# Gate and up halves of the narrow Strassen products in one PSUM bank, evicted and joined together, with a new written list of steps

## The chip, the cores and the metric

One core of a Trainium2 chip runs the whole program in one launch. The metric is the device time in microseconds, the median over runs. The change is compared with the kernel before on the same chip.

## The reference

The input is x, 2048 tokens of 512 features, with one layernorm. The output is x plus two branches of the normed tokens:

```python
xn = _layernorm(x, axis=-1)
return x + _A_ref(xn, A_wqkv, A_w_phi, A_wo) + _B_ref(xn, B_w_gate, B_w_up, B_w_down)

def _A_ref(x, wqkv, w_phi, wo):               # 32 heads of 16
    pq = jnp.einsum("bhsd,hdf->bhsf", q, w_phi)
    ...
    phi_q = jnp.concatenate([_softmax(pq, axis=-1), _softmax(-pq, axis=-1)], axis=-1)
    phi_k = jnp.concatenate([_softmax(pk, axis=-1), _softmax(-pk, axis=-1)], axis=-1)
    kv = jnp.einsum("bhsf,bhsd->bhfd", phi_k, v)
    z  = jnp.einsum("bhsf->bhf", phi_k)
    o = jnp.einsum("bhqf,bhfd->bhqd", phi_q, kv) / (phi_q . z + 1e-6)
    return o @ wo
def _B_ref(x, w_gate, w_up, w_down):          # 512 -> 1792 -> 512
    g = jnp.einsum("bsd,df->bsf", x, w_gate)
    u = jnp.einsum("bsd,df->bsf", x, w_up)
    return jnp.einsum("bsf,fd->bsd", g * u, w_down)
```

## The kernel before, in words

**Tokens and stages.** The 2048 tokens are 16 tiles of 128, four to a group of 512. After a fixed start (layernorm of tiles 0 to 3, their values, the first hidden columns) everything is a named step. The steps of every engine stand in one list, the string `ORDER`, written out by hand; the program issues them in exactly that order, and the place in each PSUM and SBUF ring is written out beside it (`SLOTS`). Nothing is scheduled at run time: each engine executes its own steps in list order and waits on semaphores.

**Names of steps.** `vk`, `q`, `kx`, `qy`, `kr` and the like are the attention projections and feature maps; `kv{n}` sums keys and values; `ab{n}` is numerator and denominator of a tile, followed by `de`, `rd` and `ot` (denominator, its reciprocal, the scaled tile `otok`, L658) and by `oT`, a DMA that transposes it. `f{n}.{i}` are the pieces of the last projection of a tile, `fs` its eviction and `fo` its store. `P1` to `P8`, `K`, `A`, `B`, `J`, `X` are the same for pairs of tiles in groups 2 and 3 (two lots of Strassen products, with `K` evictions, `J` joins at L991 and stores `X`). `S` and `t`, `wt`, `ct` prepare sums and differences that those products need.

**The hidden products.** Group 0 computes gate and up plainly (`g`, `u`, L351). For the other groups the product of tokens and gate/up weights is done by a seven-product Strassen form over halves of the features, the columns and the tokens. `block_steps(b, group)` makes the steps: block b holds one gate (b even) or one up (b odd) column pair, `k = b // 2`. For tokens 1024 to 2047 it is the wide form (512 columns to a product, steps `p1.b` to `p7.b`). For tokens 512 to 1023 it is the narrow form, with the same names behind an `N` and 256 columns to a product; it covers 14 blocks. Each product is two matmuls (L825).

In one block: product 1 fills bank `sa`, `k1` (L833) evicts it to SBUF, product 6 goes on accumulating in the same bank, `k2` evicts it, product 7 follows, `k3` evicts it, then product 4, which `d4` takes out. Products 2 and then 5, 7, 3 use banks `sb` and `sc`. The joins `j2`, `j7`, `j3` add a bank and a kept copy. In gate blocks a join writes the hidden tile `hT` (L840) and scales by `gate_scale`; in up blocks it writes `u_sb` (L844), and a step `m` multiplies that into `hT` (L847). So a gate block and its up block evict, join and multiply one after the other. A narrow product fills half of a bank; `sa` and `sc` are of the two-deep pool `f` that `=f` opens when the attention pool of `ab` closes (`bank_f`), `sb` is of the ring of six banks (`bank`).

**Engines.** The end of a word says the engine: `/a` ScalarE (ACT), `/v` VectorE (DVE), `/g` GpSimd (POOL). Joins are on the DVE. DMA triggers (`xt`, `qt`, `oT`, `fo`, `X`, `wq`) are all in the SyncE (SP) queue. Where a DVE step and a POOL step both work in SBUF, the POOL step that follows in the list waits for the DVE step (L1064 to L1084).

Of the kernel before, what the change touches and what calls it, by code (L numbers as in the profile page):

```python
# [30 lines left out]
ki4 sc12 h8 u11 vk7.0 vk7.1 kr6 ki6 n0.2 vc6/a ky5 kp4/g vc5/a kx5 kr5 xt10 n2.4 ky7 kx7 wq h11 ki5 kr7 kv4 n0.1
vk8.0 ki7 kp6/g vk8.1 vk10.0 vk10.1 g5 ky8 kx8 kp5/g kp7/g a13/a kv5 vc7/a kr8 xt11 kv6 vk9.0 vk9.1 kx10 ky10
gc5/a vc10/a vc8/v g2 kv7 ki8 a12/v kp8/g kr10 ki10 vc9/a ky9 kx9 Nz0/v fq0 xt13 a14/v vk11.0 vk11.1 fqv0/a
fqa0/a gc2/a ky11 xt12 kx11 kp10/g kv8 fq2 kr9 ki9 fqa2/v u2 q0.0 fqv2/a q0.1 kr11 ki11 qx0 qy0 q1.0 h2 q1.1
kp9/g qy1 kp11/g vk12.0 kv9 vk12.1 xt14 qx1 a15/a vc11/a kx12 kv10 ky12 qr0 qi0 qp0/g n0.6 vk13.0 vk13.1 vk14.0
# [5 lines left out]
qr4 qp5/g inv0 de2 z0/v rd2 f1.0 f1.5 f0.8 qt5 qi4 t00/g ot2 qp4/g z1/g f0.4 oT2 qx6 qy6 qy7 up60/a qr6 ab3 de3
fs0 qx7 rd3 qi6 ot3 qr7 t01/v z2/v n2.1 t02/v qp6/g f2.6 f2.1 f2.2 f2.3 p1.1 f1.6 k1.1/a f1.7 n2.0 ab5 p2.1 p1.0
f2.5 qt4 de5/a rd5 f3.0 p6.1 k1.0/a p6.0 f2.7 j2.1 f2.8 f1.8 qi7 ot5 up11/a k2.0/a t03/v p7.0 ab4 qp7/g oT3 fs2
fo0 Nz2/g q13.0 q13.1 de4/v up10/a t10/g z3/g qt6 fs1 rd4 k2.1/a wr2 p7.1 wf2 ot4 oT5 k3.0/a qx13 qy13 f3.8 qr13
qt7 p4.0 q8.0 p2.0 j2.0 ab6 p5.1 k3.1/a up50/a p4.1 de6/a rd6 p5.0 q8.1 j7.1 ot6 d4.0/a oT4 j7.0 f3.5 ab7 Np2.0
f3.7 de7/v rd7 ot7 p3.1 p3.0 up30/a qy8 up31/a m7.1/g =f t11/v qx8 j3.0 Np1.0 p1.2 Np1.1 Nk1.0/a Np6.0 j3.1
k1.2/a p2.2 Np2.1 Nj2.0 Nz3/g t12/g Nk2.0/a Nk1.1/a Nj2.1 qi13 j2.2 Np7.0 wp2 Nk3.0/a Np6.1 up20/v Nm2.1/v
m3.1/v Nk2.1/a p6.2 Np4.0 Np7.1 q9.0 Nd4.0/a Np5.0 p1.3 Nj7.0 d4.1 Nk3.1/a p2.3 Np4.1 k2.2/a k1.3/a qp13/g Np3.0
Nj3.0 p7.2 up21/a q9.1 k3.2/a Np5.1 Nd4.1 j2.3 p6.3 k2.3/a t13/g Nj7.1 p5.2 p5.3 Np1.2 qx9 Nm7.1/g fs3 Nk1.2/a
p7.3 Np2.2 Np3.1 Np6.2 p4.2 j7.2 p3.2 m2.1/v k3.3/a ws2 Nj3.1 Np1.3 j7.3 Nj2.2 t20/g m2.3/v Nk2.2/a qy9 t22/v  # L50
j3.2 Np7.2 qr8 Nk3.2/a p4.3 Nk1.3/a d4.2/a p2.4 Np4.2 Nd4.2/a Nm3.1/g t21/g t23/g Np6.3 p3.3 p1.4 Np5.2 Nj7.2
d4.3 Nk2.3/a Np7.3 p5.5 p2.5 j3.3 Np3.2 up51/a q10.0 q10.1 Nj3.2 Nk3.3/a m7.3/v up41/a k1.4/a Np5.3 p1.5 m3.3/v
Np4.3 S0.0/g t32/g j2.4 qx10 qy10 Nd4.3 Nj7.3 p6.4 k1.5/a p1.6 Np2.3 qr10 Nm7.3/v j2.5 k2.4/a Nj2.3 p6.5 Np1.4
Np3.3 p7.4 S1.0/g k2.5/a Nj3.3 p7.5 p5.4 Nm2.3/g t30/g Np2.4 k3.4/a p4.4 Nk1.4/a k3.5/a j7.4 Nj2.4 Np6.4 Np5.4
j7.5 Nk2.4/a p3.4 Np2.5 Np7.4 d4.4/a Nm3.3/v t31/g Nk3.4/a ct1.1/a p3.5 m7.5/g Np4.4 p4.5 j3.4 Nd4.4/a k1.6/a
j3.5 Nj7.4 d4.5 qi8 m2.5/v p2.7 p1.7 k1.7/a Np1.5 Np3.4 p6.6 Nj3.4 Nk1.5/a p6.7 Np6.5 k2.6/a Nk2.5/a t33/g Np5.5
Nj2.5 k2.7/a j2.7 p2.6 Np7.5 Nm2.5/v m3.5/v j2.6 S0.2/g Nk3.5/a Nj7.5 p7.6 p7.7 up40/a Np4.5 Nd4.5 k3.6/a m2.7/v
k3.7/a qp8/g Nm7.5/g oT6 p5.6 p5.7 j7.6 Np3.5 Nj3.5 Np1.6 Np2.7 Nk1.6/a p4.6 p3.6 Np6.6 Np2.6 Np1.7 j7.7 j3.6
Nj2.6 qt13 fo1 p4.7 p3.7 t40/v d4.6/a Nm3.5/v Nk1.7/a Nk2.6/a t41/v Np6.7 Np7.6 oT7 Nj2.7 m7.7/g t43/g ct2.0/a
q14.0 p1.8 Nk2.7/a p2.8 Nk3.6/a Np4.6 k1.8/a q14.1 qr9 j2.8 Nd4.6/a Np7.7 Np5.6 qi10 p1.9 p2.9 t42/g Nm2.7/g  # L60
Nj7.6 j3.7 Np3.6 Nj3.6 qx14 Nk3.7/a k1.9/a qy14 p6.8 k2.8/a j2.9 S3.0/g p6.9 Np4.7 m2.9/g Np5.7 Nd4.7 Nj7.7
k2.9/a d4.7 p7.8 p5.8 Np2.8 Np3.7 k3.8/a ct1.0/a Nm7.7/g j7.8 Np1.8 p7.9 Np2.9 Nk1.8/a p3.8 Nj3.7 Np1.9 Np6.8
p5.9 m3.7/v qp10/g k3.9/a Nk1.9/a Nj2.8 j3.8 Nj2.9 Nk2.8/a cb11.0/a j7.9 Nm3.7/v t50/v p1.11 Np7.8 p2.11 Np6.9
Nk3.8/a p3.9 Nm2.9/v wt1.0/v p4.8 Nk2.9/a Np7.9 Np4.8 t52/g t51/g j3.9 qt8 k1.11/a d4.8/a q12.0 q12.1 Nd4.8/a
Nk3.9/a p4.9 Np4.9 Np5.8 qr14 j2.11 p1.10 p2.10 p1.12 Nj7.8 Nd4.9 up61/a qx12 d4.9 wt2.0/g Np1.10 Np3.8 p5.10
m3.9/v k1.10/a Nk1.10/a Np6.10 t53/g Nj3.8 qy12 Np5.9 p2.12 j2.10 Nk2.10/a Nj7.9 m7.9/v Np7.10 t60/v Np2.10
k1.12/a Nk3.10/a Np3.9 p6.10 Np4.10 p6.11 Nj3.9 k2.10/a Nd4.10/a Nj2.10 j2.12 m2.11/g Np5.10 p7.10 q15.0 Np1.12
t62/v t61/v Nj7.10 qi9 p6.12 Np2.12 Nm7.9/g k3.10/a p4.10 Np3.10 qp9/g j7.10 qi14 Nk1.12/a k2.11/a p7.11 Nj2.12
Nj3.10 ct2.1/a p3.10 Np6.12 q11.0 S2.3/g qr12 q15.1 k3.11/a Nk2.12/a d4.10/a qy15 qx15 j3.10 Np1.11 Np7.12 t63/v
S2.2/v S0.4/v Nk1.11/a q11.1 p5.11 Np2.11 Nj2.11 j7.11 p4.11 Np6.11 Nk3.12/a Np4.12 Nd4.12/a k2.12/a d4.11 f4.7  # L70
p2.13 Nk2.11/a Np5.12 qp14/g p3.11 p7.12 qx11 qy11 Np7.11 Nj7.12 Np3.12 f6.0 Nk3.11/a qi12 S0.3/v m7.11/v qt9
f6.8 Nj3.12 j3.11 p1.13 k1.13/a k3.12/a S1.3/g Np4.11 wt2.1/v Nm2.11/v m3.11/v S2.1/v Nm3.9/g f4.2 f4.0 f6.1
Np5.11 Nd4.11 Nj7.11 qp12/g Nm7.11/g p5.12 inv1 p4.12 j2.13 Np1.13 Np3.11 j7.12 Nj3.11 qt14 Nk1.13/a d4.12/a
f6.2 f6.3 p6.13 Np6.13 p3.12 Np2.13 f4.3 k2.13/a Nk2.13/a Np7.13 Nk3.13/a Np5.13 f6.5 p7.13 qr15 S0.1/v S2.4/v
Np4.13 qt12 Nm3.11/g j3.12 Nj7.13 Nm7.13/v Nd4.13 m2.13/v S1.1/v p5.13 k3.13/a ct2.2/a f7.0 f7.1 f6.6 cb11.1/a
# [5 lines left out]
P6a.8 P5a.8 ab13 P5b.8 cb21.1/a f5.7 P2w.9 P6b.9 ct3.1/v S3.4/v oT12 fo4 qt15 oT8 fo6 P6b.8 P6b.11 P2a.9 P2b.9
A1.9/v K5.8/a K6.8/a de13/a wt3.0/v wt3.1/v P7a.8 P7b.8 f5.8 K7.8/a K6.9/a wt4.2/v J2.9 wt4.3/g A1.8/g A6.8/g
P8w.8 rd13 P5a.9 P4b.8 P4w.8 P7a.9 ot13 fs5 S3.6/v wt4.0/v ab10 oT13 fo5 S3.2/v S3.1/v P2w.8 A7.8/g P4a.8 P2a.8
P7b.9 J4.8 J8.8 de10/v K7.9/a P1b.10 B6.8/g S3.5/v rd10 A1.11/v ot10 P1a.10 P2b.8 J2.8 oT10 P3w.8 P3a.8 P3b.8
J3.8 qp11/g qt11 X8 P5b.9 A6.9/v K1.10/a K6.11/v P4w.9 P3w.9 ab15 de15/a rd15 K5.9/a A7.9/g P4b.9 X12.1 X12.0
B6.9/v ot15 P3a.9 P2b.10 P7a.11 P3b.9 P6a.10 P6b.10 P8w.9 P7b.11 K6.10/v J3.9 P4a.9 P2a.10 ab11 K7.11/a de11/a
A1.10/v J8.9 J4.9 P5a.10 P2w.10 J2.10 P3w.10 P5b.10 P3a.10 P3b.10 P4a.11 K5.10/a A6.11/g A7.11/g A6.10/g P5a.11
P5b.11 oT15 rd11 ot11 P2b.11 oT11 P4w.11 B6.10/v J3.10 K5.11/v X13.0 X10 P3a.11 P8w.10 P8w.11 X9 X13.1 B6.11/v
# [1028 lines left out]
```

## Time and profile before

| | |
|---|---|
| median of 3 runs | 211.46 us (211.44 to 211.54) |
| the profiled execution: its time, its span | 211.99 us, 210.3 us |
| PE, DVE, ACT, POOL busy | 205.2, 188.0, 152.4, 139.2 us |
| matmuls | 1463 |
| granted TensorE clock | 1.00 |
| DMA | 19.95 MB in 47,685 packets, mean 95 GB/s |

The profile is one execution. Its span is 1.7 us shorter than its own time, and that time is 0.5 us above the median of the runs. Busy PE counts a matmul to a modelled end that overlaps the next one, so short stops of the PE show only in the starts.

### The profile page before, as it was taken

Reading aid. Unit: us, or ns where it says so; the run is one execution under the profiler, and the core shown is the slowest. Engines: PE = TensorE matmul, PEld = TensorE weight load, DVE = VectorE, ACT = ScalarE, POOL = GpSimd, SP = SyncE. Lnnn points to the kernel's source line nnn. Section 1 sums busy time; section 2 is a strip of 40 time slices with the busy share of each in tenths; the row PEclk is TensorE's granted clock in tenths of the full one; section 3 lists DMA queues with packets and bytes.
Section 4 is the critical chain, followed back from the end, with each engine's and each line's share of the span. In section 5 each row is a group of like instructions: output and inputs, shape, how many; then the busy total and the mean of one; then the engine's idle time right before and its main releaser. Section 6 shows DMA issues by size and latency. Waiting matters only on the chain.

```text
span 210.3 us, 4230 instructions
## 1 busy us (share of the span) xinstructions
PE 205.2 (98%) x1463; PEld 119.8 (57%) x1463; DVE 188.0 (89%) x389; ACT 152.4 (72%) x296; POOL 139.2 (66%) x138
## 2 busy tenths in 40 slices
...
GB/s 160 261 273 380 384 315 108 86 91 53 25 61 67 0 126 99 104 145 32 15 90 0 0 3 50 0 3 3 50 50 59 19 25 125 130 75 77 77 100 75
DMA packets 47685, 19.95 MB, mean 95 GB/s; under 512 B 37424, under 2 KB 47408, under 8 KB 47536
## 3 DMA queue, kind: packets, MB, share of 16 engines
...
q8 instruction: 11, 0.18, 0.4%
q14 instruction: 10, 0.08, 0.2%
HBM read 8.67 MB, written 2.10 MB: 51 GB/s over the span
## 4 chain that ended last, share of the span: by engine, by line
PE 92%; DMA 4%; SPq 1%; DVE 1%; issue 0%; ACT 0%; DVEq 0%; ACTq 0%
PE sa L825 18%; PE fin L682 15%; PE sc L825 9%; PE q L337 7%; PE k L337 7%; PE pv L337 6%; PE u L351 6%; PE g L351 6%; PE da L962 6%; PE sb L825 4%; DMA out_dram<-o_sb 2%; DMA vk<-in_A_wqkv_dram 2%; PE dc L962 2%; PE ab L631 2%; PE kv L594 2%; PE dd L962 2%
## 5 line engine op out<-in xcount | busy, mean ns | idle before, releaser
L563 POOL TENSOR_TENSOR phik<-e,rs 128x1024 bf16<-128x1024 f32 x16 | 30.8, 1935 | 12.8 <-DVE rs L558 9.9
L553 DVE TENSOR_REDUCE sums<-e 128x64 f32<-128x1024 f32 x32 | 38.4, 1200 | 0.8 <-ACT e L541 0.4
L563 POOL TENSOR_TENSOR phiq<-e,rs 128x1024 bf16<-128x1024 f32 x16 | 30.9, 1935 | 8.4 <-DVE dK L985 1.4
L825 PEld LDWEIGHTS <-T 128*128 128x128 f16 x224 | 21.7, 98 | 15.8 <-issue 0.8
L682 PE MATMUL fin<-wd,hT 128*128 128x512 bf16 x112 | 29.4, 379 | 0.0
L357 ACT COPY k<-sa 128x512 f32<-128x512 f32 (+1 forms) x42 | 19.8, 481 | 7.4 <-PE sa L825 4.7
L359 ACT ACTIVATE k<-sa 128x512 f32<-128x512 f32 (+1 forms) x42 | 20.4, 493 | 5.0 <-PE sa L825 2.6
L825 PEld LDWEIGHTS <-wgu 128*128 128x128 bf16 x168 | 16.1, 98 | 13.0 <-DVE otok L658 0.4
L337 PEld LDWEIGHTS <-x 128*128 128x128 f16 x144 | 13.3, 98 | 13.0
L351 PEld LDWEIGHTS <-wgu 128*128 128x128 bf16 x128 | 12.3, 98 | 11.9
L558 DVE RECIPROCAL rs<-sums 128x64 f32<-128x64 f32 x32 | 17.3, 542 | 1.2
L847 POOL TENSOR_TENSOR hT<-u_sb,hT 128x256 f16<-128x256 bf16 (+1 forms) x16 | 13.1, 824 | 7.9 <-DVE wgu L932 4.3
L337 PE MATMUL pv<-vk,x 128*128 128x512 bf16 x48 | 18.2, 379 | 0.0
L337 PE MATMUL k<-vk,x 128*128 128x512 bf16 x48 | 18.2, 379 | 0.0
L682 PEld LDWEIGHTS <-hT 128*128 128x128 bf16 (+1 forms) x112 | 10.5, 98 | 9.9
L825 PE MATMUL sa<-ss,T 128*128 128x512 f16 x56 | 15.8, 379 | 0.0
L840 DVE SCALAR_TENSOR_TENSOR hT<-sc,k 128x512 f16<-128x512 f32 (+1 forms) x28 | 15.3, 545 | 0.5 <-ACT k L357 0.3
L844 DVE TENSOR_TENSOR u_sb<-sc,k 128x512 bf16<-128x512 f32 (+1 forms) x28 | 15.0, 541 | 0.3 <-POOL hT L847 0.2
L711 ACT ACTIVATE junk<-wgu 128x1024 bf16<-128x1024 bf16 x14 | 14.9, 1075 | 0.2 <-DMA x<-xn 0.2
L359 ACT ACTIVATE wgu<-wgu,up 128x1024 bf16<-128x1024 bf16 x13 | 14.9, 1158 | 0.0
L351 PE MATMUL u<-xnT,wgu 128*128 128x512 bf16 (+1 forms) x64 | 14.1, 353 | 0.0
L541 ACT ACTIVATE e<-k 128x512 f32<-128x512 f32 x24 | 13.3, 612 | 0.9 <-PE k L337 0.7
...
## 6 DMA issues: line engine op xcount, KB each, us to landing
...
xall<-in_A_x_dram SPq DMA_DIRECT2D x1, 1024.0 KB, 12.1
...
```

What stands on the lines that cost most here:

```text
L337: nc.tensor.matmul(ps, lhsT=xt(n)[:, j, :], rhs=w[:, j, :], start=(j == 0), stop=(j == DC - 1))
L351: nc.tensor.matmul(ps, lhsT=w[:, c, f * P:(f + 1) * P], rhs=(x4 if T else xnT)[:, c, lo:hi], start=(c == 0), stop=(c == DC - 1))
L357: A.copy(out=dst, in_=src)
L359: A.activation(out=dst, in_=src, func=AF.Identity, scale=scale)
L553: V.tensor_reduce(out=sums[:], in_=ev(), axis=AX.X, op=ALU.add)
L558: V.reciprocal(out=rs[:].rearrange("p a b -> p (a b)"), in_=held.pop((s + "s", n))[:])
L563: eng.tensor_tensor(out=phi[:].rearrange("p g (x f) -> p (g x) f", f=DH), in0=ev(), in1=held.pop((s + "i", n))[:].to_broadcast((P, 2 * H, ...
L682: nc.tensor.matmul(held["fin", n, lo], lhsT=l, rhs=r, start=len(done) == 1, stop=len(done) == FC + DC)
L825: nc.tensor.matmul(mine[bankname], lhsT=ww[:, j, :], rhs=xx[:, j, :], start=start and j == 0, stop=(j == hc - 1), skip_group_check=True)
L840: V.scalar_tensor_tensor(out=h(*to), in0=mine[ps], scalar=gate_scale, in1=mine[kept][:], op0=ALU.mult, op1=ALU.add)
L844: V.tensor_tensor(out=mine["u", i][:], in0=mine[ps], in1=mine[kept][:], op=ALU.add)
L962: nc.tensor.matmul(mine[ps][:, 0:W], lhsT=l, rhs=r, start=bool(mine.pop((ps, "new"), False)), stop=True, skip_group_check=True)
```

## The change

The narrow products are taken by column pair k, gate and up together, in a function of their own, `narrow_steps(k)`. A product is four matmuls: two into the left half of a bank (gate) and two into the right half (up). One eviction, one join and one `d4` of 512 elements replace two of 256 each; the joined tile `gu` holds both halves, and `Nm` multiplies one half by the other into `hT`. `Nd4` writes `gu` too, so it has an `Nm4` of its own. The levels of the two weight scales go from 8 and 8 to 4 and 4, so `gate_scale` is 1 and goes from the wide steps too: gate joins become a plain addition and gate evictions a plain copy. `u_sb` is float16. The list of steps is written anew (1156 words in place of 1247), and with it the places in the rings.

```diff
-    levels = (8.0, 8.0, 4096.0)
+    levels = (4.0, 4.0, 4096.0)
     hidden_scale = 16.0
-    gate_scale = hidden_scale / (levels[0] * levels[1])
...
+    def narrow_steps(k):
+        hc, n = DC // 2, TT // 2
+        cols = pair_cols(k)
...
+        def product(p, bankname, w, x, start=False):
+            def run():
+                if start:
+                    mine[bankname] = (bank if bankname == "sb" else bank_f)(bankname)
+                ww, xx = w(), x()
+                for g in range(2):
+                    for j in range(hc):
+                        nc.tensor.matmul(mine[bankname][:, g * n:(g + 1) * n], lhsT=ww[:, g, j, :], rhs=xx[:, j, :],
+                                         start=start and g == 0 and j == 0, stop=(j == hc - 1), skip_group_check=True)
...
+        def keep(name):
+            def run(eng):
+                mine[name] = ring(xnpool, "x", [P, TT], F32, name)
+                copy(eng, mine[name][:], mine["sa"])
...
+        def both(i):
+            mine["gu", i] = ring(gpool, "g", [P, 2, n], F16, "gu")
+            return mine["gu", i][:].rearrange("p g t -> p (g t)")
...
+        def times(i, t, f):
+            def run(eng):
+                gu = mine["gu", i]
+                eng.tensor_tensor(out=hT(1)[:, k + f * FH, t * n:(t + 1) * n], in0=gu[:, 0], in1=gu[:, 1], op=ALU.mult)
...
+        def join(i, t, f, ps, kept):
+            def run():
+                V.tensor_tensor(out=both(i), in0=mine[ps], in1=mine[kept][:], op=ALU.add)
...
+        steps[f"Nd4.{k}"] = (lambda eng: copy(eng, both(4), mine["sa"]), A)
+        times(4, 1, 0)
```

In the wide steps:

```diff
-                copy(eng, mine[name][:], mine["sa"], gate_scale if g == 0 else None)
+                copy(eng, mine[name][:], mine["sa"])
...
-                if g == 0:
-                    V.scalar_tensor_tensor(out=h(*to), in0=mine[ps], scalar=gate_scale, in1=mine[kept][:],
-                                           op0=ALU.mult, op1=ALU.add)
-                else:
-                    mine["u", i] = ring(gpool, "g", [P, n], BF16, "u_sb")
-                    V.tensor_tensor(out=mine["u", i][:], in0=mine[ps], in1=mine[kept][:], op=ALU.add)
+                if g:
+                    mine["u", i] = ring(gpool, "g", [P, TT], F16, "u_sb")
+                V.tensor_tensor(out=mine["u", i][:] if g else h(*to), in0=mine[ps], in1=mine[kept][:], op=ALU.add)
```

Places of the two lists that matter below, one of before and two of after. A word such as `p7.2` is two matmuls of 512 columns; a word such as `Np7.4` is two of 256 in the list before and four of 256 in the list after:

```
... Np7.4 d4.4/a Nm3.3/v t31/g Nk3.4/a ct1.1/a p3.5 m7.5/g Np4.4 ...

... =f Np1.0 Nk1.0/a Np5.0 k1.4/a Np2.0 qr8 Np6.0 Nk2.0/a ... p7.2 p1.3 Np7.0 ...
... P5a.10 P1a.9 cb21.1/a P5b.10 K5.10/a cb22.1/a P6a.10 ot8 K1.9/v wt4.1/v S1.6/v S3.2/v wt3.1/v S2.3/v P5a.8 P2a.8 P1a.8 K1.8/a wt4.3/v wt3.0/v P6a.9 ... P7a.10 ...
```

More of the change, by code (lines that the diff above doesn't have):

```diff
@@ L31 @@
[L31 to L35, printed above, removed]
@@ L41 @@
[L41 to L45, printed above, removed]
@@ L46 @@
[L46 to L75, printed above, removed]
@@ L81 @@
[L81 to L85, printed above, removed]
@@ L86 @@
[L86 to L90 removed]
+g3 gc3/a u3 fk0 h3 =k fk2 fka2/v fkv0/v fkv2/a g0 g1 u0 u1 gc0/v fka0/a k0 ky0 kx0 k1 k2 gc1/v h1 kx1 ky1 h0 ky2
@@ new lines @@
+Nk1.0/a Np5.0 k1.4/a Np2.0 qr8 Np6.0 Nk2.0/a t12/v fs3 j2.4 qx9 p7.2 p1.3 Np7.0 p5.2 k3.2/a t13/g m7.1/g Nj2.0
+Nm2.0/g qi8 j7.2 Nk3.0/a qy9 p2.2 m2.1/v p4.2 k1.3/a j2.2 Np4.0 p2.3 j2.3 Nd4.0/a d4.2/a p3.2 p6.3 up40/a p5.3
+Np1.1 p1.5 Nj7.0 Nz3/g Np2.1 k2.3/a Np3.0 p7.3 Nm4.0/g t20/v m2.3/v Nk1.1/a t21/v Nm7.0/v qp8/g p6.4 Np6.1 j3.2
+Nj3.0 p2.5 Np1.2 up31/a Nk2.1/a Np7.1 Nj2.1 q10.0 q10.1 k1.5/a qr9 p6.5 k3.3/a Nm3.0/g Nm2.1/g t22/g j2.5 j7.3
+Nk3.1/a wr2 wf2 qx10 wp2 qr13 m7.3/v m2.5/v Np4.1 Nk1.2/a Nd4.1 qy10 k2.4/a p3.3 p4.3 Np2.2 Np6.2 Np5.1 j3.3
@@ new lines @@
+Nj7.1 up51/a p7.4 p5.4 q14.0 t23/g Nm4.1/g d4.3 t30/v k3.4/a Np3.1 Nj3.1 up41/a Nm7.1/g Nk2.2/a q14.1 p4.4 p1.7
+Np5.2 j7.4 t31/g qi13 Nm3.1/g Nj2.2 Nm2.2/v p3.4 k2.5/a Np7.2 p7.5 p1.6 j3.4 d4.4/a Nk3.2/a Nj7.2 k3.5/a k1.7/a
+p5.5 k1.6/a j7.5 qp13/g m3.3/v p2.6 Np4.2 p6.7 Np3.2 p4.5 Nd4.2/a Nm7.2/v m7.5/v p6.6 p3.5 Nj3.2 Np5.3 Np1.3
+d4.5 qx14 up60/a k2.6/a Nk1.3/a j2.6 Np2.3 p5.6 j3.5 t32/g t33/g Nm4.2/v m3.5/v p7.6 p2.7 Nj2.3 t40/g t41/g
+Nm3.2/g k2.7/a qy14 k3.6/a qi9 Np6.3 p1.8 p7.7 j2.7 j7.6 qr10 p2.8 Nk2.3/a k3.7/a qp9/g p4.6 d4.6/a p3.6 j3.6
@@ new lines @@
+k1.8/a j2.8 Np7.3 Nk3.3/a p4.7 p5.7 p1.9 p6.8 j7.7 p2.9 k1.9/a q12.0 p3.7 Np4.3 p6.9 t42/v m2.7/v m7.7/v d4.7
+Nm2.3/g up50/a t50/g k2.8/a Nd4.3 Nj7.3 k2.9/a q12.1 j3.7 Nm7.3/v p5.9 Nm4.3/v oT6 fo2 Np3.3 t51/g Nj3.3 j2.9
+Nm3.3/v Np1.4 p7.9 p5.8 p7.8 qy12 Nk1.4/a S0.1/v t43/v k3.9/a qx12 j7.9 m3.7/v ws2 Np2.4 Nj2.4 m2.9/g k3.8/a
+j7.8 Np5.4 Nm2.4/v t52/v ct2.3/g m7.9/g Np6.4 Nk2.4/a p4.9 p4.8 d4.8/a d4.9 Np7.4 p2.10 p3.9 p1.10 Nk3.4/a
+up61/a Np4.4 Nd4.4/a k1.10/a p3.8 Nj7.4 p1.11 p2.12 Np1.5 Np3.4 Nm7.4/g j3.8 j3.9 m3.9/v p6.10 Nk1.5/a k1.11/a
@@ new lines @@
+k2.10/a t53/g j2.10 p5.10 Np6.5 p2.11 p1.12 Nj3.4 S0.0/v t60/v t61/g Nm3.4/g inv1 j2.11 Nk2.5/a p7.10 k3.10/a
+k1.12/a Np7.5 qi10 j7.10 p6.11 j2.12 k2.11/a f6.3 Nm4.4/v S0.2/v m2.11/v Np5.5 p6.12 p3.10 p7.11 Nk3.5/a Nj7.5
+f6.4 Np4.5 Np2.5 p4.10 fo0 qt13 qr14 j3.10 Nj2.5 qp10/g t63/g Nd4.5 k3.11/a f6.0 Np3.5 Nm2.5/v Np1.6 p1.13 p5.11
+p4.11 f6.8 d4.10/a cb11.0/a k1.13/a p6.13 Nk1.6/a Nm7.5/v S0.4/v Np6.6 S2.1/v Nm4.5/v cb11.1/a j7.11 ct2.1/a
+Nj3.5 d4.11 p3.11 q15.0 q15.1 j3.11 qi14 t62/g m7.11/g p2.13 f6.2 qt9 oT7 j2.13 Nk2.6/a Np5.6 Np2.6 Nm3.5/g
@@ new lines @@
+qp14/g f6.5 f4.0 qx15 qy15 k2.12/a k2.13/a qt8 p7.12 ct1.0/a Nj2.6 qr12 S0.3/v Np7.6 f6.1 q11.0 k3.12/a Nk3.6/a
+Nm2.6/g qi12 Nj7.6 Nm7.6/g qp12/g qt12 p7.13 p5.12 q11.1 j7.12 qr15 p4.12 Np3.6 p3.12 Nj3.6 j3.12 f4.3 ct1.1/a
+qx11 k3.13/a f4.1 d4.12/a Nm3.6/v p5.13 p4.13 qy11 Np4.6 m2.13/v S0.5/v f6.7 f4.5 f4.4 f5.8 f7.3 Nd4.6/a f4.7
+f4.8 =ab2 wt1.0/v m3.11/v Nm4.6/v S2.5/v S2.4/v j7.13 S1.2/g ct2.0/a d4.13 S1.1/v wt2.0/v wt1.1/v ct2.2/a qt14
+S1.4/g ab9 de9/a rd9 ot9 qi15 f7.1 f6.6 f4.6 f7.8 f5.7 f5.0 oT9 qt10 f5.6 P1b.9 f5.2 f5.5 ab14 S1.3/v f7.4 f7.5
```

136 lines of the change are left out of this document (86 added, 50 removed).

## The prediction

> **What bounds the kernel.** I read the page first (busy times), then the table by windows, the groups with shapes kept apart, the timeline of the PE around its stops, and the waits.
>
> ```profile
> PE 205.2 (98%) x1463; PEld 119.8 (57%) x1463; DVE 188.0 (89%) x389; ACT 152.4 (72%) x296; POOL 139.2 (66%) x138
> ```
>
> ```profile
> 110.00:120.00 10.00, 9.95 (x57) 5.42 (x56) 9.91 (x22) 8.53 (x18) 7.96 (x8) 1.00 0.00 0
> 130.00:140.00 10.00, 10.00 (x62) 5.95 (x61) 9.94 (x22) 9.54 (x21) 8.10 (x8) 1.00 0.01 2
> 190.00:200.00 10.00, 9.60 (x100) 8.51 (x98) 7.18 (x17) 2.55 (x6) 4.52 (x5) 1.00 0.45 81
> ```
>
> The columns are start and end, length, then busy time of PE, PE weight load, DVE, ACT, POOL, then clock and DMA. The PE is the bound in every stretch, at full clock; the DVE is nearly full beside it from 110 to 140.
>
> How much can be won? Starts in the timeline lie 0.216 us apart for 512 columns, 0.109 for 256 and 0.033 for the 68 of `ab` and `kv`. The groups count 636, 488 and 256 of these: 137.4 + 53.2 + 8.4, and about 2.2 for the transposes and folds, make 201.2 us of pure streaming. The PE starts at 0.83 and ends at 207.17, 206.3 us. So 5.1 us are lost: 3.2 before 13.8 us, at the start, which stands ahead of the list; about 0.4 in the folds (`f{k,q}`, about 0.1 before and after 32 small matmuls), which stay; and ten stops later. By the starts these are 0.15 us at 77.7, 0.21 at 95.2, 0.11 at 97.1, 0.05 at 99.1, 0.07 at 111.8, 0.18 at 115.7, 0.20 at 118.7, 0.07 at 132.9, 0.07 at 145.8 and 0.57 at 198.3, together 1.67 us. One of them (PE, then ACT):
>
> ```profile
> 117.86 0.38 PE L825 MATMUL sa<-s,T 128*128 128x256 f16 x2
> 118.08 0.59 PE L825 MATMUL sc<-ss,wgu 128*128 128x512 f16 x2
> 118.72 0.81 PE L825 MATMUL sa<-x,T 128*128 128x256 f16 x4
> ```
>
> ```profile
> 118.28 0.38 ACT L359 ACTIVATE k<-sa 128x256 f32<-128x256 f32 x1 [0.21 <-PE sa L825]
> ```
>
> This is `Np7.4`, `Nk3.4`, `p3.5`, `Np4.4`. Two matmuls of 256 stream until 118.08, the eviction starts 0.20 later, takes 0.38, and about 0.04 after it bank `sa` is free: 0.63 us. The list puts only `p3.5` between, 0.43 us. Calculated loss 0.20, seen 0.20. The last stop is another kind:
>
> ```profile
> PE dc L962 <- DVE o_sb L991: 0.4, 1, 0.4
> DVE o_sb L991 <- DMA out_dram<-o_sb: 3.1, 2, 1.7
> ```
>
> A join waits for an output tile whose store has not landed, and a product waits for the bank that the join empties.
>
> **What the change does to the PE.** The order of instructions has 1463 matmuls of the same shapes in both kernels. No streaming goes. A gain comes from stops alone: at most 1.67 us of 211.46, plus 0.12 at 13.2 us, where the first fold waits for the DVE's `bd`; in the new list `u3` (0.86 us) comes ahead of the folds.
>
> **What it does to the other engines.** The rows:
>
> ```profile
> L359 ACT ACTIVATE k<-sa 128x512 f32<-128x512 f32 x21 | 12.6, 600 | 2.4 <-PE sa L825 1.7 <-DVE u_sb L844 0.6
> L359 ACT ACTIVATE k<-sa 128x256 f32<-128x256 f32 x21 | 8.1, 386 | 2.5 <-PE sa L825 0.9 <-DVE u_sb L844 0.5 <-DVE hT L857 0.5
> L844 DVE TENSOR_TENSOR u_sb<-sc,k 128x512 bf16<-128x512 f32 x14 | 9.4, 673 | 0.0
> L844 DVE TENSOR_TENSOR u_sb<-sc,k 128x256 bf16<-128x256 f32 x14 | 5.7, 410 | 0.3 <-POOL hT L847 0.2
> L847 DVE TENSOR_TENSOR hT<-u_sb,hT 128x256 f16<-128x256 bf16 x10 | 2.9, 288 | 0.0
> ```
>
> Narrow work on the DVE before: 42 joins of 0.41, seven `Nd4` of 0.42 and ten `Nm` of 0.29, 23.0 us; back-to-back instructions start 0.08 us earlier than these durations say, so 18.3. After: 21 joins of 0.67 and 14 `Nm` of 0.29, 18.2, less 0.08 each, 15.4. The DVE wins 2.9 us. ACT before: 49 of 0.38; after: 28 of 0.60; less 0.10 each, 13.7 and 13.9: nothing. POOL: 11 `Nm` become 14 at 0.67, 2 us more. float16 in place of bfloat16 and a copy in place of a scaled copy (600 against 589 ns) I cost at nothing. All of it lies beside the PE; its worth is what the list makes of it.
>
> **What the new list makes of it.** For each matmul that waits for another engine I took the spare: from the end of the last PE word that the awaited chain needs, in streaming time of the words between, less 0.20, the durations of the chain and 0.04 a handover; queues on those engines are left out. In the list before, 250 such waits behind the start have 17 under 0.1 us (three below zero) and 41 under 0.25. In the new list 247 have 7 under 0.1 (one at zero) and 9 under 0.25. Five of the nine stops from 77.7 to 145.8 lie at waits of the 17 and lose 0.50 us. The other four (77.7, 95.2, 111.8, 115.7; 0.61 us) wait for `otok` or a join that stood behind others on the full DVE, and the DVE has 2.9 us less to do. By kind: a narrow eviction of before needs 0.63 us of other PE work between two products in `sa`; of 42, one has 0.43 and seven have 0.65. The new one needs 0.20 + 0.60 + 0.04 = 0.84; of 21, four have 0.86 (`Nk1.0`, `Nk2.0`, `Nk2.1`, `Nk2.4`), the others 1.30 or more. The seven are these four, `ab7` behind its `otok`, and two `K` of pair 10.
>
> New stops, bounded by 0 and by 2.2 us (a third more than all the old): 0.04 at each of the seven, about what the old sites with 0.02 to spare lost, 0.30; and 0.15 in the pair stage. I take 0.45, near the low end, because these sites are the nearest rows.
>
> Stores: the three stores of before that took 3.6 to 4.3 us were issued behind a transpose still in flight (193.28 to 194.37). In the new list `X12.1`, `X8`'s neighbours and `X14` are released by joins at 184 to 186 us of streaming, ahead of `qt15`, some 3.4 us before joins take their tiles; the 64 KB stores at the end took 1.5 to 1.8. So I count the 0.57 as won. If they meet a transpose (4.3), 0.9 us on the DVE comes back, of which the PE saw a fifth before. Elsewhere SP's queue moves nothing late: the closest transpose, `oT11`, has 3.7 us from its issue to `P2w.11`, against 2.4 to 3.5 taken. The end is as before: a last quarter join, a store and the close, 3.1 us behind the last matmul.
>
> Sum: -1.67 - 0.10 + 0.45 = -1.32. Of the profiled execution's 211.99 us that leaves 210.7; of the median, 0.53 lower, 211.46 - 1.32 = 210.1. About 0.2% (0.42 us) is what a measurement of this kernel can tell from no change.
>
> **Rivals.** *Longer evictions decide (slower).* A merged product gives its bank up 0.21 us later than a half did (597 against 386 ns), and four sites have 0.02 us to spare. If ACT, busy 8.5 to 9.5 us of 10 here, is in an instruction of 0.48 each time a product ends, these four cost 0.46 each, 1.84 us: 210.1 + 1.8 = 212.0. It decides from 0.44 us a site on. For it: the spare is less than any instruction. Against it: what the list puts on ACT ahead of these four (`up31` of 1.16 at the worst) is done, by the same sums, before the product ends, and before 8 of 42 sites were as tight and lost 0.2 at most. The Trainium skill, Perfetto Trace Analysis, section Optimizing Scalar/DVE Operations, speaks for this rival: where these engines are not saturated but cause bubbles on others, it advises to break instructions up, the opposite of this change. By that rule the trace agrees for ACT (bubbles at 118.7), not for the DVE, which is full.
>
> *New shortfalls as large as the old.* A list with good margins can still lose where durations differ from the rows or a DMA is late; 1.6 us of such stops give 211.3. Against it: of 233 waits of before with over 0.1 us to spare four stopped the PE, by 0.61 us in all, with the DVE fuller than it will be.
>
> *The DVE in the pair stage.* The new list moves eight `S` sums and four `wt` pieces from POOL to the DVE and four `S` back. From the release at 168.9 to `wt3.0`, which `P7a.10` awaits at 178.9, stand 21 instructions of 10.7 us; less 0.08 each and with 0.5 of waiting they end at 178.4, 0.45 us to spare. Eleven are 16-bit SBUF operations; the rows of L932 go from 362 to 605 ns. At 0.19 more each, 2.1 us, the PE waits 1.6: 211.7. For: POOL works beside them. Against: their median is 413.
>
> That the halves are not joined as said is no rival: the order shows 21 evictions and 21 joins of 512 where 42 of 256 stood.
>
> **Numbers.** Margins hold, 210.1 (own range 209.5 to 210.9): 0.64. Longer evictions, 212.0: 0.13. New shortfalls, 211.3: 0.13. DVE in the pair stage, 211.7: 0.10. The low end has no new stop (209.7) and 0.2 for the start; the high end, 211.9, takes in the middle cases and leaves out about half of the slow one. Faster by over 0.2%: 0.64 and 0.05 of the shortfalls, 0.69. Within: 0.06 of the shortfalls, 0.06 of the DVE, 0.02 of the evictions, 0.14. Slower: 0.02, 0.04 and 0.11, 0.17.
>
> **What would show it.** PE starts after 14 us with stops of about 0.45 us beside the folds, none over 0.2; no wait of PE for `o_sb`; DVE busy about 181 to 184 us, ACT within 2 us of 152, POOL about 140. The eviction rival would show stops of 0.3 or more in front of `Np6.0`, `Np7.0`, `Np7.1`, `Np7.4`; the DVE rival one in front of a `da` product near 184 us. I am wrong if stops sum to over 1.3 us, or if streaming itself takes longer.

## The result, and the profile after

| | before | after |
|---|---|---|
| median | 211.45 us (211.05 to 211.86, 22 runs) | 210.87 us (210.56 to 211.32, 22 runs) |
| ratio, 95% interval | 1 | 0.9974 (0.9967 to 0.998) |
| traced execution: time, span | 211.99, 210.3 us | 211.32, 209.6 us |

The change makes the kernel 0.58 us faster (0.42 to 0.70 by the interval). Forecast was 1.32: the sign is right, the size more than twice too large.

The busy times of the page after:

```profile
PE 204.9 (98%) x1463; PEld 120.0 (57%) x1463; DVE 184.2 (88%) x361; ACT 154.2 (74%) x279; POOL 140.1 (67%) x141
```

The engines beside the PE moved about as forecast: the DVE is 3.8 us lighter (the sum had 2.9, for its narrow work alone), ACT 1.8 us heavier (the sum had nothing, the signs "within 2"), POOL 0.9 (the sum had 2).

The windows in which the old stops lay (columns as before), and two that now hold new ones, at 30 and at 90 us:

```profile
30.00:40.00 10.00, 9.78 (x60) 4.54 (x58) 9.76 (x21) 9.27 (x19) 8.57 (x11) 1.00 1.16 163
90.00:100.00 10.00, 9.92 (x71) 4.69 (x68) 9.49 (x19) 9.24 (x17) 9.71 (x8) 1.00 0.60 120
110.00:120.00 10.00, 10.00 (x67) 6.28 (x65) 9.51 (x17) 9.09 (x17) 7.91 (x12) 1.00 0.00 0
130.00:140.00 10.00, 10.00 (x61) 5.86 (x60) 9.81 (x25) 8.16 (x15) 4.75 (x6) 1.00 0.34 66
190.00:200.00 10.00, 10.00 (x109) 9.02 (x106) 6.92 (x19) 2.07 (x5) 7.28 (x8) 1.00 0.47 104
```

The PE is full from 110 to 200. The waits of the PE after, the whole list (total, times, longest):

```profile
PE warm L371 <- PEq L1151: 0.8, 1, 0.8
PE pv L331 <- DMA vk<-in_A_wqkv_dram: 0.5, 1, 0.5
PE pv L331 <- DMA x<-xn: 0.2, 1, 0.2
```

No product waits for `o_sb` any more. A transpose of an input tile does show up, 0.2 us by this list, which counts from the modelled end of the matmul before. By the starts it is more:

```profile
35.97 0.38 PE L331 MATMUL k<-vk,x 128*128 128x512 bf16 x1
36.56 0.39 PE L331 MATMUL pv<-vk,x 128*128 128x512 bf16 x1 [0.22 <-DMA x<-xn]
```

Starts lie 0.59 us apart where 0.216 would do: 0.38 us lost. This is `vk5.0`, waiting for `xt5`. Two of the four sites with 0.02 us to spare, `Np6.0` at 101.36 and `Np7.0` at 102.70, in the PE's timeline:

```profile
100.92 0.60 PE L880 MATMUL sb<-x,wgu 128*128 128x256 f16 x4
101.36 0.60 PE L880 MATMUL sa<-s,T 128*128 128x256 f16 x4
101.80 0.59 PE L815 MATMUL sa<-ss,T 128*128 128x512 f16 x2
102.23 0.59 PE L815 MATMUL sa<-x,wgu 128*128 128x512 f16 x2
102.70 0.61 PE L880 MATMUL sa<-s,T 128*128 128x256 f16 x4
```

Groups of two or four start 0.43 to 0.44 us apart; only in front of `Np7.0` are there 0.03 us too many. All ten old stops are gone, and with them three of 0.03 to 0.04 us at 98.0, 110.9 and 116.4 (0.12 us together) that the prediction did not list. New beside the folds are 0.06 us at 25.1, 0.38 at 36.6, 0.24 at 98.1 and 0.03 at 102.7, together 0.72 us, where the prediction's signs were about 0.45 us and none over 0.2.

### The profile page after: what moved, and what is told of

The parts are those of the page before. It is cut to its first block, busy times and chain, and to the rows that moved or that the text cites. A ratio compares the mean times of both kernels' runs of the same rounds, so it can differ in the third digit from the quotient of the medians.

```text
span 209.6 us, 4165 instructions
## 1 busy us (share of the span) xinstructions
PE 204.9 (98%) x1463; PEld 120.0 (57%) x1463; DVE 184.2 (88%) x361; ACT 154.2 (74%) x279; POOL 140.1 (67%) x141
## 4 chain that ended last, share of the span: by engine, by line
PE 87%; DMA 4%; POOL 3%; issue 2%; DVE 2%; SPq 1%; ACT 1%; POOLq 0%; ACTq 0%
PE fin L676 15%; PE sa L815 12%; PE da L1012 7%; PE pv L331 7%; PE q L331 7%; PE sa L880 6%; PE sc L815 6%; PE k L331 5%; PE sc L880 3%; PE u L345 3%; PE sb L815 3%; PE dc L1012 2%; PE dd L1012 2%; PE db L1012 2%; DMA x<-xn 2%; PE g L345 2%
## 5 line engine op out<-in xcount | busy, mean ns | idle before, releaser
L351 ACT COPY k<-sa 128x512 f32<-128x512 f32 x63 | 35.2, 593 | 6.6 <-PE sa L880 3.8
L345 PEld LDWEIGHTS <-wgu 128*128 128x128 bf16 x128 | 12.2, 98 | 11.3 <-issue 0.2
L353 ACT ACTIVATE wgu<-wgu,up 128x1024 bf16<-128x1024 bf16 x14 | 16.0, 1161 | 0.5 <-DVE up L733 0.5
L815 PE MATMUL sa<-ss,T 128*128 128x512 f16 x56 | 16.3, 379 | 0.0
L768 POOL TENSOR_TENSOR T<-wgu,T 128x512 f16<-128x512 bf16 x11 | 12.7, 1158 | 4.4 <-DVE T L768 2.2
L535 ACT ACTIVATE e<-q 128x512 f32<-128x512 f32 x24 | 14.0, 615 | 1.5 <-PE q L331 1.4
L345 PE MATMUL g<-xnT,wgu 128*128 128x512 bf16 (+1 forms) x64 | 13.9, 352 | 0.0
L331 PE MATMUL q<-W1q,x 128*128 128x512 bf16 x48 | 13.5, 379 | 0.0
```

Source lines behind the costliest of these rows:

```text
L331: nc.tensor.matmul(ps, lhsT=xt(n)[:, j, :], rhs=w[:, j, :], start=(j == 0), stop=(j == DC - 1))
L345: nc.tensor.matmul(ps, lhsT=w[:, c, f * P:(f + 1) * P], rhs=(x4 if T else xnT)[:, c, lo:hi], start=(c == 0), stop=(c == DC - 1))
L351: A.copy(out=dst, in_=src)
L353: A.activation(out=dst, in_=src, func=AF.Identity, scale=scale)
L535: A.activation(out=held[s + "e", n][:, :, sign, :], in_=held[s, n].rearrange("p (g c) -> p g c", g=NG), func=AF.Exp, scale=(nrst if sign e ...
L815: nc.tensor.matmul(mine[bankname], lhsT=ww[:, j, :], rhs=xx[:, j, :], start=start and j == 0, stop=(j == hc - 1), skip_group_check=True)
```

## Experiments

Times are medians; a ratio is to the kernel before, run beside it on the same chip. Traces with 1442 or 1445 matmul records miss some; gaps of exactly one such matmul (0.216 us) are counted as that matmul, not as stops.

### The last stop of before: e4, e5, e9, e13

e4 edit:

```diff
-    "o": "0120201201001120",
+    "o": "012020120100120",
...
-                    mine["o", t] = ring(opool, "o", [P, D], BF16, "o_sb")
+                    mine["o", t] = (early.tile([P, D], BF16, name="o_sb", tag="vk") if t == 15
+                                    else ring(opool, "o", [P, D], BF16, "o_sb"))
```

> The kernel before, with one edit: the output tile of token tile 15 lies in the place of the long dead wv/W1k instead of the third ring place that tile 10's store still holds. Theory: the stop of 0.57 us at 198.3 (store, then join, then bank) goes, and the time falls by 0.5 to 0.57 us, to 210.9: then this one stop is worth as much as the whole change was measured to be, and the other nine stops that the change took away (1.10 us) were eaten by its new ones and its start. Rival: the next link is as late (that product's bank or the join's other operand): under 0.2 us of gain.

Measured: 211.50, ratio 0.9998 (0.9989 to 1.0007), against before's 211.56: nothing won, and a gain of 0.5 us lies outside the interval. But the edit does not touch the stop that it was meant for. These are the two waits for a store in before:

```profile
197.73 0.48 DVE L991 SCALAR_TENSOR_TENSOR o_sb<-dd,inv,dK 128x256 bf16<-128x256 f32 x1 [1.39 <-DMA out_dram<-o_sb]
203.82 0.48 DVE L991 SCALAR_TENSOR_TENSOR o_sb<-dd,inv,dK 128x256 bf16<-128x256 f32 x1 [1.68 <-DMA out_dram<-o_sb]
```

By the order of the joins in the list, which the banks in the timeline follow, the first is `J8.9`, the first join of tile 13. Tile 13 takes the ring place of tile 8, and the join starts 0.12 us after tile 8's store `X8` lands (issued at 193.28, landed at 197.61); tile 10's store is issued only at 201.96. The second is `J8.11`, the first join of tile 15, in the place of tile 10. So e4's edit takes away the wait at 203.8, and nothing is won by that: in before, the PE has no stop there. The wait of `J8.9` is missing from e4's trace because `X8` took 2.5 us in that execution in place of 4.3 and was done in time:

```profile
196.29 0.48 DVE L992 SCALAR_TENSOR_TENSOR o_sb<-dd,inv,dK 128x256 bf16<-128x256 f32 x1
```

That traced execution takes 211.45 us, 0.54 less than the traced one of before. For the stop at 198.3, e4 is one more trace of the kernel before, with no stop in it; neither theory nor rival is tested.

e5 is the kernel before again, for a second trace.

> The kernel before, unchanged, for a second profile. The first took 211.99 us against a median of 211.45, and taking its store stop away (e4) moved the median by nothing. Theory: the stop of 0.57 us at 198.3 belongs to that execution and not to the kernel; a second profile has it at under 0.2, a span of about 209.7, and the other nine stops as they were (1.1 us in all). Rival: the stop is there again at 0.5 to 0.6 in a span of 210.2 or more; then e4's edit brought another loss in its place, and the 0.54 between profile and median lies elsewhere.

Measured: 212.01 us, span 210.3, the store stop 0.24 us, the start 0.34 us later than in the first trace, the other nine stops 1.11 us. Theory and rival each hold in part: the stop is smaller, the time is not.

e9 is the same kernel with timed executions.

> The kernel before, unchanged, this time with its own timed executions, so that one list holds the traced execution and the others. Traced twice it took 211.99 and 212.01 us, in both with a wait for a store at 198.3 (0.57 and 0.24 us, the second after a start 0.33 us later), while its median is 211.44 to 211.56. Theory: the wait for the store is long only in the traced execution; that one takes 212.0 again and the others 211.3 to 211.6, and the 0.57 us of the prediction's sum was never in the median. Rival: the traced one is like the others this time (211.3 to 211.6), the stop is small in it, and the two earlier ones were chance.

Measured: the traced execution 211.87, the other eleven 211.17 to 212.23 around 211.66. Neither reading holds as stated. The store wait is in the trace again (0.41 us by the starts):

```profile
PE dc L962 <- DVE o_sb L991: 0.2, 1, 0.2
DVE o_sb L991 <- DMA out_dram<-o_sb: 2.9, 2, 1.7
```

Executions of this kernel scatter more (standard deviation 0.33 us) than e4's (0.14 us, 211.28 to 211.74); the medians, from two chips, lie 0.2 us apart. The kernel before that ran beside e9 has a median of 211.50: two lots of the same kernel on one chip differ by as much.

e13 takes the output tiles of tiles 14 and 15 out of the ring (`late_o()[:, t - 14, :] if t > 13`, one early tile for both). Tile 13 stays in it.

> The kernel before with the output tiles of token tiles 14 and 15 both in the place of the long dead wv/W1k, so that neither of the two joins that waited for a store (1.39 us of DVE at 197.7, 1.68 us at 203.8) waits. Theory: the waits show at 0.24 to 0.65 us of PE in the traces of before, but the median of the timed executions holds hardly any of it, as e4 gave: 0 to 0.2 us under before. Rival: e4's second wait (203.8) took back what the first gave; without both the median falls by the 0.4 to 0.55 us of the traces.

Measured: 211.59, ratio 1.0003 (0.9992 to 1.0014). The wait at 203.8 is gone from the trace, with no gain. `J8.9` still waits for `X8` (landed at 196.81), and the PE loses 0.20 us:

```profile
196.93 0.48 DVE L999 SCALAR_TENSOR_TENSOR o_sb<-dd,inv,dK 128x256 bf16<-128x256 f32 x1 [1.01 <-DMA out_dram<-o_sb]
```

What follows: no run here takes tile 13 out of tile 8's place, so no experiment takes the stop away. Six traces of before and its near copies (before, e5, e9, e10 below, e13 and e4) have it at 0.57, 0.24, 0.41, 0.65, 0.20 and 0 us, 0.35 on average. How much of it the timed executions hold was not measured. An estimate: in each of the six, the traced time less the store stop and less what the PE has lost by the first fold (2.8 to 3.6 us, 3.2 on average) is 208.2 us (208.19 to 208.22). The median of 211.45 leaves 3.25 us for the two, and so about 0.1 us for the stop, if timed executions start like the traced ones, which no run shows. The prediction's 0.57 came from one execution, near the upper end.

### The wait for tile 5's transpose: e1, e2, e6, e14, e15, e10, e11

e1 is the changed kernel again, e14 a third time.

> The changed kernel as it is, for a second profile and as the yardstick of the three beside it. Theory A (the late start in the first profile of the changed kernel is chance: the load of wv landed at 5.45 us there and at 4.77 in the profile of before, with the same instructions ahead of it): the PE has lost between 3.0 and 3.4 us by 14.6 us this time, the stops after it are again 0.38 us near 36.5, 0.24 near 98 and four of 0.1 in the folds, and the time is 210.9 +-0.2. Theory B (something in the new kernel makes the start later each time): 3.6 us again by 14.6 us.

Measured: 211.01, ratio 0.9976 (0.9967 to 0.9985). Theory A: by the first fold the PE has lost 3.0 us, against 3.65 in the first trace after and 3.2 in the first of before. In the eleven traces of kernels with the new list it is 2.9 to 3.65 us; the first trace after is the latest of them by 0.44 us. The stop at 36 us is 0.58 us here, not 0.38.

> The changed kernel, unchanged, as the yardstick for e15 on one chip and with a third trace: 210.9 +-0.15, stops of 0.35 to 0.6 at 36 us and of 0.25 at 98 us, nothing over 0.05 at the four tight sites.

Measured: 210.84, ratio 0.9967 (0.9955 to 0.9979); stops of 0.52 at 36.0 and 0.24 at 97.5 us.

e2 edit:

```diff
-a7/a xt4 a6/g xt6 xt5 g11 ...
+a7/a xt4 a6/g xt5 xt6 g11 ...
```

> The changed kernel with xt5 ahead of xt6 on SP's queue, nothing else moved. Theory: the stop of 0.38 us at 36.56 is tile 5's transpose, third on SP's queue behind those of tiles 4 and 6 (issued 29.31, 30.60, 31.86; landed 34.19, 34.68, 36.52), while vk5.0 is ready for it at 36.2. As the second it lands about 34.7, vk5.0 does not wait, and the time falls by 0.35 to 0.4 us to about 210.5. Rival: the queue's transposes are late because the loads of wd and wo (until 33.03) or the long transpose wq share the DMA engines with them; then the stop moves to vk4.0 or vk6.0/vk7.0 and the time stays within 0.1 of e1.

Measured: 211.38, ratio 0.9992 (0.9983 to 1.0): 0.37 us slower than e1, worse than either reading. ACT and PE in its timeline:

```profile
36.11 1.06 ACT L705 ACTIVATE junk<-wgu 128x1024 bf16<-128x1024 bf16 x1 [1.51 <-DMA x<-xn]
```

```profile
37.29 0.38 PE L331 MATMUL pv<-vk,x 128*128 128x512 bf16 x1
38.28 0.38 PE L331 MATMUL k<-vk,x 128*128 128x512 bf16 x1 [0.61 <-ACT e L535]
```

`vk5` runs on without a stop. But the weight norm `n1.5` writes its `junk` into the ring place that tile 6's `xn` holds until `xt6` has read it. With `xt6` third, ACT waits 1.51 us, evicts tile 4's `k` late, and `vk7` waits 0.78 us for that bank. The order that the list had was the better one: both transposes were late.

e6 edit (the load leaves the head of SP's queue):

```diff
-    nc.sync.dma_start(out=wo[:], in_=A_wo.rearrange("(c p) n -> p c n", p=P))
...
+    @step("wo")
+    def _():
+        nc.sync.dma_start(out=wo[:], in_=A_wo.rearrange("(c p) n -> p c n", p=P))
...
-... vk6.0 xt9 xt10
+... vk6.0 xt9 xt10 wo
```

> The changed kernel with the load of wo taken from the head of SP's queue and issued behind xt10 (about 42 us), its first use being far later. Theory: the transposes of tiles 4 to 7 are held up by the loads of wd and wo, which land at 31.6 and 33.0 us (the first transpose takes 4.9 to 5.1 us from issue to landing, later ones 2.4); without wo's 512 KB in front they land about 1.4 us earlier, vk5.0 finds xt5 there and ACT finds tile 6's buffer free, the stop of 0.38 to 0.58 near 36 goes, and the time is 0.4 to 0.6 us under e1, about 210.5. Rival: the transposes go one after the other at their own pace (about 1.3 us of issue each) and xt5, the third, is late whatever was loaded before: no change, 211.0.

Measured: 210.37, ratio 0.9948 (0.9937 to 0.996). Issue to landing of the first three transposes: 3.4, 2.5 and 2.5 us, against 4.9, 4.1 and 4.7 in the first trace after. In PE's timeline the fifth tile follows the fourth without a break:

```profile
35.18 0.38 PE L330 MATMUL pv<-vk,x 128*128 128x512 bf16 x1
35.40 0.38 PE L330 MATMUL k<-vk,x 128*128 128x512 bf16 x1
```

The theory holds: the stop came from a 512 KB load that nobody needed yet, ahead of the transposes. In all five kernels here with the new list and `wo` late, the third transpose takes 2.5 us, and no stop at 36 us is left (0.09 us at 37.5 in e12); with `wo` early and the list's own order it took 4.7 to 4.9 us in four traces. A new one of 0.22 us shows at 43.5 in e6's trace.

> The kernel of e6 beside the changed kernel on the same chip. Theory: the stop at 36 us is worth in the median what the traces show, 0.4 to 0.6 us; with it gone the change as a whole would have been worth 1.0 to 1.1 us. Rival: as with the store, traces show more than the median holds: under 0.3 us between e14 and e15.

Measured: 210.57, ratio 0.9954 (0.994 to 0.9967), 0.27 us under e14. By its letter that is the rival's reading (under 0.3), where the traces of the two differ by 0.41 us; six executions each do not tell 0.27 from 0.4. Its trace has no stop between 33 and 60 us but the folds. With e6 and e11 the kernels with `wo` late lie 0.9 to 1.1 us under before by their means, the changed kernel 0.6 in three runs: the stop is worth 0.3 to 0.5 us in timed executions.

e10 puts the same load late in the kernel before (`xt11 wo kv6`).

> The kernel before with the load of wo issued behind xt11 (as e6 does for the changed kernel). In before the first transpose lands at 33.17 and vk4.0 stands at 35.4 us, and no stop shows between 14 and 50 us. Theory: nothing waits there, so nothing is won: within 0.15 us of before. Then the stop that e6 took away was one that the new list made by drawing vk4 and vk5 forward by 1 us. Rival: an earlier landing helps in both kernels (the loads disturb more than the transposes): 0.3 us or more faster.

Measured: 211.68, ratio 1.001 (0.9999 to 1.0021): nothing is won. The stop needs both: the load ahead, and the new list, which runs `vk4` 1 us earlier and `vk5` directly behind it.

e11 is e6 with `ky7` ahead of `a12` on ACT.

> e6 with ky7 ahead of a12 on ACT. In e6 a stop of 0.22 us was left at 43.45: the bank of tile 7's k waits for ky7, which stands on ACT behind a12 (0.8 us, itself waiting 0.5 us for POOL's nb). Theory: the stop goes and the time falls to 0.2 us under e6, 0.7 us under the changed kernel (ratio to before about 0.994). Rival: xt12 comes 0.6 us later by it and vk12 or POOL's next step waits instead: as e6.

Measured: 210.49, ratio 0.995 (0.9938 to 0.9962). Its trace has no stop at 43.5, and its traced execution is the fastest here (210.26), but the median is e6's. e15 shows no such stop without this edit: it was not there to be won each time. e6, e11 and e15 are faster than both kernels compared here.

### The ab7 site: e3, e7

e3 is e2 with `f3.5` moved from behind `ab7` to ahead of it.

> As e2, and the PE step f3.5 (0.43 us) moved from behind ab7 to ahead of it. Theory: ab7 waits 0.24 us for otok of tile 6 on the DVE with nothing ready between; f3.5 covers it, the stop near 98 goes, 0.2 to 0.25 us under e2, about 210.3, the best of the four. Rival: ab7 now begins 0.2 us later, the DVE's den, reciprocal and otok of tile 7 with it, and since the DVE is full here the 0.2 comes back as stops between 98 and 115 us: the same time as e2.

Measured: 211.21, ratio 0.9986 (0.9976 to 0.9996), about e2. The stop moved by one wait for `otok`:

```profile
97.75 0.42 PE L625 MATMUL ab<-KV,phiqT 128*128 128x68 bf16 x8
98.01 0.59 PE L815 MATMUL sb<-x,wgu 128*128 128x512 f16 x2
98.44 0.59 PE L815 MATMUL sa<-ss,T 128*128 128x512 f16 x2
98.87 0.59 PE L815 MATMUL sa<-x,wgu 128*128 128x512 f16 x2
99.63 0.61 PE L880 MATMUL sa<-x,wgu 128*128 128x256 f16 x4 [0.17 <-DVE otok L652]
```

`ab7` starts at once, but `Np1.0` uses the place of `ab`'s banks and needs tile 7's `otok` out of them: 0.33 us.

e7 is e6 with both gaps filled:

```diff
-k1.2/a qt7 ot6 ab7 d4.1 t11/g Nz2/g m3.1/g up21/a n2.5 oT4 fo1 de7/v rd7 ot7 f3.5 p2.4 p6.2 k2.2/a p1.4 =f Np1.0
-Nk1.0/a Np5.0 k1.4/a Np2.0 qr8 Np6.0 Nk2.0/a t12/v fs3 j2.4 qx9 p7.2 p1.3 Np7.0 p5.2 k3.2/a
+k1.2/a qt7 ot6 f3.5 ab7 d4.1 t11/g Nz2/g m3.1/g up21/a n2.5 oT4 fo1 de7/v rd7 ot7 p2.4 p6.2 k2.2/a p1.4 Np2.0 =f Np1.0
+Nk1.0/a Np5.0 k1.4/a t12/v p7.2 qr8 Np6.0 Nk2.0/a fs3 j2.4 qx9 p1.3 p5.2 Np7.0 k3.2/a
```

> As e6, and the list eased at the ab7 site as a whole: f3.5 goes ahead of ab7 (as in e3), Np2.0 ahead of the change of banks that waits for otok of tile 7, and t12, p7.2 and p5.2 one or two places up, so that Np6.0 and Np7.0 keep a product between an eviction and the next use of its bank. Theory: e3 only moved the stop (0.25 at 97.6 became 0.33 at 99.6, both behind an otok), since the pair ab6, ab7 and the change of banks ask for 1.8 us of other PE work twice and the list had 1.7; with one step more in each the stops of 0.25 and 0.04 go, and the time is 0.2 to 0.3 us under e6. Rival: p7.2 moved up waits for t12 on the full DVE, 0.2 to 0.4 us at 101 to 102 us, and nothing is won.

Measured: 210.63, ratio 0.9958 (0.9946 to 0.997), no better than e6. Both stops behind `otok` are gone; `p1.3` now waits 0.26 us for the bank that `fs3` empties and `p5.2` 0.17 us for its own. The rival's place is right, not its cause (`t12`).

### What merging itself is worth: e8, e12

e8 keeps list and banks, and makes each eviction and join in two:

```diff
-                copy(eng, mine[name][:], mine["sa"])
+                for g in range(2):
+                    copy(eng, mine[name][:, g * n:(g + 1) * n], mine["sa"][:, g * n:(g + 1) * n])
...
-                V.tensor_tensor(out=both(i), in0=mine[ps], in1=mine[kept][:], op=ALU.add)
+                to = both(i)
+                for g in range(2):
+                    h = slice(g * n, (g + 1) * n)
+                    V.tensor_tensor(out=to[:, h], in0=mine[ps][:, h], in1=mine[kept][:, h], op=ALU.add)
```

> The changed kernel and its list with the 21 evictions of 512 and the 21 joins of 512 of tokens 512 to 1023 each made as two of 256 again; banks, tiles, products and the order stay. The DVE gets 21 x 62 ns = 1.3 us more (two of 0.331 back to back for one of 0.600), ACT 21 x 56 ns = 1.2 us. Theory of the prediction (the gain is the slack that merging gives the DVE, spent by the list): at the four tight sites (0.02 us to spare) the bank comes free about 0.06 to 0.15 us later, so stops of 0.05 to 0.15 each show in front of Np6.0, Np7.0, Np7.1 and Np7.4, and some on the DVE between 110 and 130: 0.3 to 0.8 us slower than e1. Rival (the list alone makes the gain, merging is not needed): within 0.15 us of e1. The Trainium skill's rule (Perfetto Trace Analysis, Optimizing Scalar/DVE Operations: break instructions up where they make bubbles on others) would have it no slower, or faster.

Measured: 211.12, ratio 0.9985 (0.9976 to 0.9995), 0.1 to 0.2 us slower than e1. DVE is busy 185.0 us, 0.8 more. The places are as the sums of spare said; `Np6.0` at 100.94 and `Np7.0` at 102.33:

```profile
100.43 0.60 PE L880 MATMUL sb<-x,wgu 128*128 128x256 f16 x4
100.94 0.60 PE L880 MATMUL sa<-s,T 128*128 128x256 f16 x4
101.37 0.59 PE L815 MATMUL sa<-ss,T 128*128 128x512 f16 x2
101.80 0.59 PE L815 MATMUL sa<-x,wgu 128*128 128x512 f16 x2
102.33 0.61 PE L880 MATMUL sa<-s,T 128*128 128x256 f16 x4
```

0.51 and 0.53 us between starts for 0.44: 0.07 and 0.09 us lost, then 0.03 at 110.2 and 138.0.

> e11 with the 21 evictions and 21 joins of 512 split into halves as in e8, so that the worth of the merging is seen without the stop at 36 us, which was 0.42 in e8's trace and 0.58 in e1's. Theory: 0.15 to 0.3 us slower than e11 (e8's trace has new stops of 0.07 at 100.9, 0.09 at 102.3 and of 0.03 at 110.2 and 138.0, 0.2 us in all, against none to 0.04 in e1). Rival: no slower than e11, and what e8 lost against e1 is scatter.

Measured: 210.61, ratio 0.9953 (0.994 to 0.9966), 0.1 us over e11, within the scatter. Its trace has the same stops as e8's (0.07, 0.09, 0.03). By the traces merging is worth about 0.2 us; the medians leave open anything from 0 to 0.4. The rest of the change's worth comes with the list and what else e8 and e12 keep (banks, scales, types); no run takes these apart.

## Why the prediction was right and wrong

**Held.** Streaming is unchanged. The nine stops from 77.7 to 145.8 us (1.10 us) went and stayed away in every trace of the new list. The counted spare was exact enough to name the places: four sites with 0.02 us left lost 0.04 at most, and with two evictions in place of one 0.03 to 0.09. The rival of longer evictions is thereby refuted. The Trainium skill, Perfetto Trace Analysis, section Optimizing Scalar/DVE Operations, advises both: larger operations where an engine is saturated, smaller ones where it is not saturated but makes bubbles on others. Here the runs agree with the first half (DVE 88% busy, 0.8 us more with the pieces apart); breaking the pieces up again (e8) brought more bubbles, not fewer. The pair stage shows no stop; the 0.15 us set aside for it was not needed.

**Failed: "Elsewhere SP's queue moves nothing late".** This step put the wait for an input tile's transpose at nothing. It asked how far the closest transpose stands from its user and allowed 2.4 to 3.5 us for the transfer. `xt5` had 4.3 us (issued at 31.86, `vk5.0` ready at 36.2), more than was allowed for, and took 4.7; `xt4` and `xt6` took 4.9 and 4.1, all behind the load of `wo`. The trace of before already had 3.9 and 3.7 us for the first two transposes behind that load, and the step left these rows out. It cost 0.38 to 0.58 us in the traces and 0.3 to 0.5 in the medians, and moving the load took it away (e6, e11, e15). That is about half of the 0.74 us by which the measured gain falls short of the forecast one.

**Mis-sized: the store stop.** "So I count the 0.57 as won" took the size of one execution for that of the kernel. The stop is gone, as forecast: no product waits for `o_sb` in any trace of the new list. But in six traces of before it is 0 to 0.65 us, and the median holds about 0.1 of it by the estimate above. So some 0.2 (by the mean of the traces) to 0.5 us (by the estimate) of the forecast gain were not there to be won; which of the two stays open, since no run takes the stop away. The reason given for the long stores, a transpose still in flight, does not decide it either: in e4 the same transpose is in flight, and `X8` takes 2.5 us.

"Of the median, 0.53 lower" carried the gap between traced execution and median over as a constant. It came out nearly so (0.45), by luck: in before the gap goes with the store stop, while the traced execution of after has no such stop and starts 0.44 to 0.75 us later than the other ten of the new list.

**Mis-sized: the new stops in the list.** `ab7` was named as a site with no spare and costed at 0.04; it lost 0.24 to 0.25 in each trace of a list that keeps its place. The links of that chain (ACT, then DVE, then the PE) in the trace after:

```profile
96.35 0.38 ACT L636 ACTIVATE den<-ab,eps,inv 128x32 f32<-128x32 f32 x1
```

```profile
96.80 0.34 DVE L647 RECIPROCAL rden<-den 128x32 f32<-128x32 f32 x1
97.23 0.69 DVE L652 TENSOR_TENSOR otok<-ab,rden 128x512 bf16<-128x512 f32 x1
```

```profile
98.07 0.41 PE L625 MATMUL ab<-KV,phiqT 128*128 128x68 bf16 x8
```

From one end to the next start pass 0.07, 0.09 and 0.15 us where the sum had 0.04 for each: that is 0.19 of the 0.24. The other six sites lost next to nothing. And the 0.10 counted for the first fold, which no longer waits for `bd`, was 0.03: the fold has a stop of 0.095 in front of it in any case (0.125 before). The parts that the prediction gives for the 5.1 us lost (3.2, 0.4 and 1.67) add up to 5.3, and the three small stops come on top; the forecast does not hang on that sum.

Put right: -1.10 - 0.12 (the three small stops) - 0.1 (the store, the estimate) - 0.03 + 0.24 + 0.09 (25.1 and 102.7 us) + 0.3 to 0.5 (`xt5`) is -0.7 to -0.5 us, against -0.58 measured. With 0.35 for the store, the mean of the traces, it would be -1.0 to -0.8. That speaks for the smaller figure without proving it.
